# Linear attention with a gated FFN on one core: load gates read a ScalarE marker of each step instead of the newest FFN product

## The chip, the cores and the metric

The kernel runs on one core of a Trainium2 chip. The metric is the device time of one execution in microseconds: 285.78 us before the change (median of 3 runs, 285.7 to 285.8). A profiled execution, from whose trace all stretches below are read, spans 284.2 us between its first and its last instruction.

The core has five engines that run side by side, each through its own instructions in order: TensorE (PE in the profile; its weight loads are the row PEld), VectorE (DVE), ScalarE (ACT), GpSimd (POOL) and SyncE (SP). Transfers run on 16 DMA engines. An instruction that needs another engine's result waits for a semaphore, and all that stands behind it on its own engine waits too.

## The reference

```python
def phi(x, c, s):
    r = np.maximum(x, 0.0)
    return np.concatenate([r * c, r * s], axis=-1)
q_p = phi(q, cos_w, sin_w)
k_p = phi(k, cos_w, sin_w)
kv = np.einsum('bhsf,bhsd->bhfd', k_p, v)
z = np.sum(k_p, axis=2)
num = np.einsum('bhsf,bhfd->bhsd', q_p, kv)
den = np.einsum('bhsf,bhf->bhs', q_p, z)[..., None] + 1e-06
x = (num / den)            # to (B*S, H*D) = (4608, 512)
a = x @ w1
b = x @ w2
h = a * b @ w3
out = h @ w_out
```

q, k and v are 8 batches x 8 heads x 576 positions x 64. w1 and w2 are 512 x 1024, w3 is 1024 x 1024, w_out is 1024 x 512. All inputs and the output are float32.

## The kernel before

**Blocks and slots.** The FFN runs in nine blocks of 512 tokens (t=0 to 8), written by `ffn_groups` (line 426). A block of t=1 or more has 24 steps, called slots: 16 product slots (x times a piece of w1, `aT`, and x times the same piece of w2, `bT`, in turn, for eight pieces) and 8 output slots (four outputs of 128 tokens, two slots each). w3 times w_out is multiplied once, in t=0, as `w34b`, so an output is one product of `abT` with `w34b`. Slots 0 to 39 are t=0, and t begins at slot 16+24t: t=1 at 40, t=2 at 64, t=3 at 88, t=4 at 112, t=5 at 136, t=6 at 160, t=7 at 184, t=8 at 208.

In a product pair ScalarE copies the first product from PSUM to `asb` (line 470, one of three buffers) and VectorE multiplies it with the second into `abT` (line 475). There are four PSUM buffers `ffnps` for these. An output is copied by ScalarE (line 497) to `osb`, or, for the first ten pairs of outputs, to `kept`, which is stored much later.

**Attention between the slots.** At each slot the kernel calls what a hand-written plan has put there (`at`, `plan`, lines 522 to 543), and these instructions follow those of the slot on their engines. A batch of attention goes through: loads of k, v and q, each in two pieces (`load`, line 109: 64 partitions with 320 positions, then 64 with 256, converted to bf16); features of k and q on VectorE and ScalarE (lines 259 and 263); values copied by GpSimd (line 283); the product of keys and values (line 291) and its copy `kvs`; the transpose `qpT` of the query features by DMA (line 277, issued by SP); the numerator `pnum` on TensorE (line 349); its division (lines 359 to 361) into `xblk`; and the transpose of that into the block's input `xT` by DMA (line 383, SP). The plan gives slots for all of them: `kf` for key features, `vc` for values, `kv` for the key-value product, `qf` for query features, `nu` for numerators and the xT transpose behind each. A batch has five pieces of up to 128 positions, so five slots for each. For batches 4 to 7 all slots are given relative to a base: 101, 127, 153, 178. Batch b has 576 tokens and blocks have 512, so t=3 needs the first three pieces of batch 3, t=4 the first two of batch 4, t=5 the first two of batch 5, t=7 the first of batch 7.

**Loads and their gates.** All loads of k, v and q after the first batch, and the stores of `kept` and most of `osb`, are issued by GpSimd. Keys and values have one buffer, queries two. A load piece could be issued long before its slot, since GpSimd has little else to do. So each is put behind a gate (`behind`, line 525): GpSimd copies one column of a tile to `seen`, and can't do so before that tile is written. `plan_loads` (line 545) uses the newest `asb`, kept in `last_product` (lines 460 and 471); so do the ten late stores (lines 619 to 623). `plan_loads` is called ahead of `plan` for the same batch, so at a shared slot the load stands first.

Of the kernel before, what the change touches and what calls it, by code (L numbers as in the profile page):

```python
# [11 lines left out]
BF16 = mybir.dt.bfloat16  # L12
# [4 lines left out]
P = 128  # L17
# [3 lines left out]
ROWS = [128, 128, 128, 128, 64]  # L21
# [47 lines left out]
def kernel(  # L69
# [11 lines left out]
    nc = tc.nc  # L81
# [10 lines left out]
    sm = ctx.enter_context(tc.tile_pool(name="sm", bufs=3))  # L92
# [59 lines left out]
    zeros = const.tile([P, 512], BF16, name="zeros")  # L152
# [68 lines left out]
    def w34_mm(jp, part):  # L221
        if part == 0:
            w34_acc[jp] = ffn_tile()
        acc, w3T = w34_acc[jp], w3Ts[jp]
        for lc in range(4 * part, 4 * part + 4):
            nc.tensor.matmul(acc[:, :], lhsT=w3T[:, lc, :], rhs=woutb[:, lc, :],  # L226
                             start=(lc == 0), stop=(lc == 7))
        if part == 1:
            nc.scalar.copy(out=w34b[:, jp, :], in_=acc[:, :])


    def order_of(b):

        return [0, 1, 2, 3, 4] if b % 2 == 0 else [4, 0, 1, 2, 3]
# [5 lines left out]
    feat = {}  # L240
# [29 lines left out]
    def prep_k(b, c):  # L270
        features(b, feat_of(b)[0], raw[b, "k"], c)
# [149 lines left out]
    def ffn_tile():  # L421
        pool = ps_ffn[ffn_tiles[0] // 2 % 2]
        ffn_tiles[0] += 1
        return pool.tile([P, 512], FP32, name="ffnps")

    def ffn_groups(t):
        x = xT[t]
        abT = fsb.tile([P, 8, 512], BF16, name="abT", bufs=2)

        def products(out, w, jc, tok):  # L430
            for kc in range(4):
                nc.tensor.matmul(out, lhsT=w[:, kc, ts(jc, 128)], rhs=x[:, kc, tok],  # L432
                                 start=(kc == 0), stop=(kc == 3))

        def on_half(half):

            for pair in range(2):
                a, b = ffn_tile(), ffn_tile()
                if pair == 0 and t == 0:
                    for quarter in range(2):  # L440
                        for i in range(2):
                            for ps, w in ((a, w1b), (b, w2b)):
                                products(ps[:, ds(256 * i + 128 * quarter, 128)], w, i,
                                         ds(256 * half + 128 * quarter, 128))
                            if half == 0 and quarter == 0 and i == 0:
                                yield
                        if quarter == 0:
                            yield
                else:
                    for ps, w in ((a, w1b), (b, w2b)):  # L450
                        for i in range(2):
                            products(ps[:, ts(i, 256)], w, 2 * pair + i, ts(half, 256))
                        if w is w1b and (t == 1 or half == 0):
                            yield
                asb = fsb.tile([P, 512], BF16, name="asb")
                nc.scalar.copy(out=asb[:], in_=a[:, :])
                nc.vector.tensor_mul(out=abT[:, ts(pair, 2), ts(half, 256)],
                                     in0=asb[:].rearrange("p (i n) -> p i n", i=2),
                                     in1=b[:, :].rearrange("p (i n) -> p i n", i=2))
                last_product[:] = [asb]  # L460
                yield

        if t < 2:
            yield from on_half(0)
            yield from on_half(1)
        for jc in range(4 if t < 2 else 0, 8):
            aT = ffn_tile()
            products(aT[:, :], w1b, jc, slice(0, 512))
            asb = fsb.tile([P, 512], BF16, name="asb")
            nc.scalar.copy(out=asb[:], in_=aT[:, :])  # L470
            last_product[:] = [asb]
            yield
            bT = ffn_tile()
            products(bT[:, :], w2b, jc, slice(0, 512))
            nc.vector.tensor_mul(out=abT[:, jc, :], in0=asb[:], in1=bT[:, :])  # L475
            yield
        if t == 0:
            for jp in range(8):
                for part in range(2):
                    w34_mm(jp, part)  # L480
                    yield
            early.close()
            holds.append(ctx.enter_context(tc.tile_pool(name="hold", bufs=HELD,
                                                        reuse_waits="tile")))
        for ms in range(3 if t == NT - 1 else 4):
            ops = ffn_tile()
            for jc in range(8):
                nc.tensor.matmul(ops[:, :], lhsT=abT[:, jc, ts(ms, 128)], rhs=w34b[:, jc, :],  # L488
                                 start=(jc == 0), stop=(jc == 7))
                if jc == 3:  # L490
                    yield
            if ms % 2 == 0:
                if len(held) < HELD:
                    osb = holds[0].tile([P, 2, 512], FP32, name="kept")
                else:
                    osb = fsb.tile([P, 2, 512], FP32, name="osb", bufs=2)
            nc.scalar.copy(out=osb[:, ms % 2, :], in_=ops[:, :])  # L497
            if t == NT - 1:
                store(nc.sync, osb[:, ms % 2:ms % 2 + 1, :], 4 * t + ms, 1)
            elif ms % 2 == 1:  # L500
                if len(held) < HELD:
                    held.append((osb, 4 * t + ms - 1))
                else:
                    store(nc.gpsimd, osb[:, :, :], 4 * t + ms - 1, 2)
            yield
        if t == NT - 1:
            for half in range(2):
                cols = ts(half, 256)
                ops = ffn_tile()
                for jc in range(8):  # L510
                    nc.tensor.matmul(ops[:, 0:256], lhsT=abT[:, jc, ts(3, 128)],  # L511
                                     rhs=w34b[:, jc, cols], start=(jc == 0), stop=(jc == 7))
                nc.scalar.copy(out=osb[:, 1, cols], in_=ops[:, 0:256])  # L513
                store((nc.sync, nc.scalar), osb[:, 1:2, :], 4 * t + 3, 1, cols)
                yield
# [6 lines left out]
    def at(s, *calls):  # L522
        slots[s] += calls

    def behind(what):

        seen = sm.tile([P, 1], BF16, name="seen", bufs=1)
        nc.gpsimd.tensor_copy(out=seen[0:what.shape[0], :], in_=what)  # L528

    def feature_of(b, i, c):  # L530
        return feat[b][i][0:ROWS[c], c, 0, 0:1]

    def plan(b, kf, vc, kv, qf, nu, loads=None, xt=None):
        order = order_of(b)
        for i, c in enumerate(order):
            at(kf[i], lambda c=c: prep_k(b, c))
            at(qf[i], lambda c=c: prep_q(b, c))
            at(vc[i], lambda c=c: prep_v(b, c))
        for i, c in enumerate(order):
            at(kv[i], lambda c=c, i=i: kv_chunk(b, c, i))  # L540
        for i, c in enumerate(order):
            at(nu[i], lambda c=c: num(b, c))
            at(xt[i] if xt else nu[i], lambda c=c: x_tr(b, c))

    def plan_loads(b, when):

        for piece, s in zip([(n, half) for n in "kvq" for half in range(2)], when):
            def issue(piece=piece):
                behind(last_product[0][:, 0:1])
                load(b, *piece)  # L550
            at(s, issue)

    last_product = []

    for c in range(NCH):
        prep_k(0, c)
# [44 lines left out]
    for c, s in zip(order_of(1), (31, 32, 33)):  # L601
# [2 lines left out]
    plan(2, kf=(33, 35, 37, 39, 40), vc=(41, 42, 43, 44, 45), kv=(45, 46, 46, 47, 47),  # L604
         qf=(40, 41, 42, 43, 44), nu=(48, 50, 52, 54, 57))
    plan_loads(3, (51, 53, 55, 57, 59, 61))
    plan(3, kf=(58, 60, 62, 63, 65), vc=(62, 63, 64, 65, 66), kv=(72, 73, 73, 74, 74),
         qf=(67, 69, 71, 73, 75), nu=(75, 77, 79, 82, 85))

    bases = {4: 101, 5: 127, 6: 153, 7: 178}  # L610
    for b, base in bases.items():
        plan_loads(b, [base - 26 + s for s in (3, 5, 7, 9, 12, 14)])
        plan(b, kf=[base + s for s in (-16, -14, -12, -10, -9)],
             vc=[base + s for s in (-12, -11, -10, -9, -8)],
             kv=[base + s for s in (-3, -2, -2, -1, -1)],
             qf=[base + s for s in (-8, -6, -4, -2, 0)],
             nu=[base + s for s in (0, 2, 4, 7, 10)])

    for i in range(HELD):
        def put(i=i):  # L620
            behind(last_product[0][:, 0:1])
            store(nc.gpsimd, held[i][0][:, :, :], held[i][1], 2)
        at(166 + 4 * i, put)

    g = 0
    for t in range(NT):
        for _ in ffn_groups(t):
            for u in slots[g]:
                u()
            g += 1  # L630
# [31 lines left out]
```

## Time and profile before

| | |
|---|---|
| time | 285.78 us (285.7 to 285.8) |
| span of the profile | 284.2 us |
| TensorE busy | 253.0 us, 89% |
| VectorE, ScalarE, GpSimd busy | 137.9, 126.7, 91.9 us |
| mean granted TensorE clock | 0.952 |
| DMA | 41.01 MB, 144 GB/s |
| gate copies `seen<-asb` on GpSimd (line 528) | 46, 201 ns each |

Columns of a group or timeline line are engine, source line, operation, what is written and read, shapes and count; in brackets stands how long the engine was idle before it and what ended that. A wait line gives the waiting engine and line, what it waited for, then total us, times, and the longest. A chain line gives start, duration and what. The two digit rows of the page cut the span into 40 slices of 7.1 us, in tenths.

### The profile page before, as it was taken

The numbers are of one execution on the slowest core, as the hardware profiler recorded it, in microseconds if no ns is written. First come the engines' busy times: TensorE is split into PE (matmuls) and PEld (weight loads), VectorE is DVE, ScalarE is ACT, GpSimd is POOL, SyncE is SP. The second block draws the span as 40 slices with busy tenths as digits, with TensorE's granted clock in tenths as the row PEclk, the third lists the DMA queues.
The fourth block names the chain that finished last, engine by engine and source line by source line (L and its number), as shares of the span: only waits on it lengthen the run. The fifth ranks groups of instructions, "written<-read, shape, count | busy, mean of one in ns | idle before, by whom it ended". The sixth has DMA issues, their size and how long they took to land.

```text
span 284.2 us, 4962 instructions
## 1 busy us (share of the span) xinstructions
PE 253.0 (89%) x1867; PEld 133.3 (47%) x1867; DVE 137.9 (49%) x330; ACT 126.7 (45%) x218; POOL 91.9 (32%) x191
## 2 busy tenths in 40 slices
PE   8789999989999998999699949999868718999993
PEld 3577555649654543454245414454324303444442
DVE  6774736468772473465265614565524312521420
ACT  2774236758337624572456314663434301324331
POOL 8573403213064022504060302508246520454000
PEclk9999999999999999999989986999995966999999
DMA  8999999994699679978985994679998992767005
GB/s 192 187 194 205 206 208 144 196 123 74 132 147 169 77 124 166 137 137 119 149 96 97 144 124 59 82 148 162 167 196 211 174 248 74 164 155 237 0 17 131
DMA packets 83894, 41.01 MB, mean 144 GB/s; under 512 B 51488, under 2 KB 80416, under 8 KB 83872
## 3 DMA queue, kind: packets, MB, share of 16 engines
q0 software_dynamic: 35456, 27.20, 62.6%
q1 hardware_dynamic: 48256, 13.38, 31.6%
q8 instruction: 14, 0.23, 0.3%
q10 hardware_dynamic: 160, 0.13, 0.2%
q14 instruction: 8, 0.07, 0.1%
HBM read 38.80 MB, written 9.44 MB: 170 GB/s over the span
## 4 chain that ended last, share of the span: by engine, by line
PE 35%; DMA 19%; ACT 2%; issue 1%; DVE 1%; POOL 0%; ACTq 0%; SPq 0%; POOLq 0%
PE ffnps L432 26%; DMA xT<-xblk 9%; PE ffnps L488 6%; DMA qpT<-qp 4%; DMA qs<-in_q_dram 3%; DMA ks<-in_k_dram 3%; PE pnum L349 1%; PE pnum L291 1%; ACT asb L470 1%; ACT qp L263 0%; DVE kvs L297 0%; POOL out_dram L417 0%; ACT kvs L296 0%; PE ffnps L511 0%; ACT osb L513 0%
## 5 line engine op out<-in xcount | busy, mean ns | idle before, releaser
L432 PE MATMUL ffnps<-xT,w1b 128*128 128x512 bf16 (+2 forms) x336 | 78.6, 361 | 14.8 <-DMA xT<-xblk 12.9
L432 PE MATMUL ffnps<-xT,w2b 128*128 128x512 bf16 (+2 forms) x336 | 78.7, 361 | 4.6 <-DVE abT L475 4.6
L475 DVE TENSOR_TENSOR abT<-asb,ffnps 128x512 bf16<-128x512 bf16 x64 | 43.9, 685 | 65.1 <-PE ffnps L432 62.8
L488 PE MATMUL ffnps<-w34b,abT 128*128 128x512 bf16 x280 | 67.0, 384 | 0.0
L470 ACT CAST asb<-ffnps 128x512 bf16<-128x512 f32 x64 | 37.3, 583 | 65.8 <-PE ffnps L432 52.9
L432 PEld LDWEIGHTS <-w1b 128*128 128x128 bf16 x336 | 31.4, 100 | 45.3 <-DMA xT<-xblk 11.4
L432 PEld LDWEIGHTS <-w2b 128*128 128x128 bf16 x336 | 31.5, 100 | 34.7 <-issue 10.2
L528 POOL COPY seen<-asb 128x1 bf16<-128x1 bf16 x46 | 9.2, 201 | 96.4 <-ACT asb L470 96.4
L488 PEld LDWEIGHTS <-abT 128*128 128x128 bf16 x280 | 25.7, 99 | 26.6 <-issue 1.1
L263 ACT ACTIVATE qp<-qs,sinv 128x512 bf16<-128x512 bf16 (+2 forms) x40 | 28.0, 717 | 10.0 <-DMA qs<-in_q_dram 6.5
L361 DVE TENSOR_TENSOR xblk<-pnum,den 128x512 bf16<-128x512 f32 (+1 forms) x39 | 27.0, 691 | 1.4
L263 ACT ACTIVATE kp<-ks,sinv 128x512 bf16<-128x512 bf16 (+1 forms) x35 | 25.0, 722 | 3.7 <-DMA ks<-in_k_dram 3.7
L497 ACT COPY kept<-ffnps 128x512 f32<-128x512 f32 x20 | 11.7, 585 | 25.9 <-PE ffnps L488 25.9
L349 PEld LDWEIGHTS <-qpT 128*128 128x128 bf16 x320 | 15.2, 100 | 15.5 <-issue 5.1
L283 POOL COPY va<-vs 128x512 bf16<-128x512 bf16 (+1 forms) x30 | 17.6, 630 | 14.3 <-DMA vs<-in_v_dram 12.0
L349 PE MATMUL pnum<-kvs,qpT 128*128 128x65 bf16 x312 | 16.9, 196 | 3.8 <-DMA qpT<-qp 2.6
L497 ACT COPY osb<-ffnps 128x512 f32<-128x512 f32 x15 | 8.8, 585 | 24.6 <-PE ffnps L488 24.6
L259 DVE TENSOR_SCALAR qp<-qs,cosv 128x512 bf16<-128x512 bf16 (+1 forms) x40 | 14.3, 366 | 8.8 <-DMA qs<-in_q_dram 8.8
L359 DVE TENSOR_SCALAR den<-pnum 128x8 f32<-128x8 f32 (+1 forms) x39 | 6.4, 164 | 24.0 <-PE pnum L349 24.0
L259 DVE TENSOR_SCALAR kp<-ks,cosv 128x512 bf16<-128x512 bf16 (+1 forms) x35 | 15.8, 473 | 3.5 <-DMA ks<-in_k_dram 3.5
L417 POOL DMA_DIRECT2D out_dram<-osb x18 | 9.6, 536 | 20.3 <-ACT osb L497 19.2
L226 PE MATMUL ffnps<-woutb,w3T 128*128 128x512 bf16 x64 | 15.0, 379 | 0.0
(84 smaller groups left out, 196.1 us busy)
## 6 DMA issues: line engine op xcount, KB each, us to landing
out_dram<-kept POOLq DMA_DIRECT2D x10, 256.0 KB, 4.3
qs<-in_q_dram POOLq DMA_DIRECT2D x9, 256.0 KB, 7.8
ks<-in_k_dram POOLq DMA_DIRECT2D x7, 320.0 KB, 5.3
qs<-in_q_dram POOLq DMA_DIRECT2D x7, 320.0 KB, 9.0
vs<-in_v_dram POOLq DMA_DIRECT2D x7, 320.0 KB, 9.9
ks<-in_k_dram POOLq DMA_DIRECT2D x7, 256.0 KB, 6.0
vs<-in_v_dram POOLq DMA_DIRECT2D x7, 256.0 KB, 9.2
out_dram<-osb POOLq DMA_DIRECT2D x6, 256.0 KB, 4.3
```

What stands on the lines that cost most here:

```text
L226: nc.tensor.matmul(acc[:, :], lhsT=w3T[:, lc, :], rhs=woutb[:, lc, :], start=(lc == 0), stop=(lc == 7))
L259: nc.vector.tensor_scalar(out=dst[:R, c, :, 0:D], in0=src[:R, :, c, :], scalar1=0.0, scalar2=cosv[:R, at:at + 1], op0=ALU.max, op1=ALU.mult)
L263: nc.scalar.activation(out=dst[:R, c, 0:n, D:F], in_=src[:R, 0:n, c, :], func=ACTF.Relu, scale=sinv[:R, at:at + 1], bias=0.0)
L283: eng.tensor_copy(out=feat_of(b)[2][:R, c, :, 0:D], in_=raw[b, "v"][:R, :, c, :])
L349: nc.tensor.matmul(nt[:, h // 4, ds((h % 4) * 65, 65)], lhsT=qpT[:, h, ds(at, 128)], rhs=kvs[:, h, :], start=True, stop=True)
L361: nc.vector.tensor_tensor(out=xblk[rows], in0=n4[:, :, :, 0:D], in1=den[rows].unsqueeze(3).to_broadcast([R, 2, 4, D]), op=ALU.mult)
L417: on.dma_start(out=rows[:, :, cols], in_=osb[64 * i:64 * i + rows.shape[0], :, cols])
L432: nc.tensor.matmul(out, lhsT=w[:, kc, ts(jc, 128)], rhs=x[:, kc, tok], start=(kc == 0), stop=(kc == 3))
L470: nc.scalar.copy(out=asb[:], in_=aT[:, :])
L475: nc.vector.tensor_mul(out=abT[:, jc, :], in0=asb[:], in1=bT[:, :])
L488: nc.tensor.matmul(ops[:, :], lhsT=abT[:, jc, ts(ms, 128)], rhs=w34b[:, jc, :], start=(jc == 0), stop=(jc == 7))
L497: nc.scalar.copy(out=osb[:, ms % 2, :], in_=ops[:, :])
```

## The change

Each gate gets its own marker: ScalarE copies one element of a tile of zeros into `mark`, and GpSimd copies that. The marker depends on no data; it is ready when ScalarE, which works in order, has come to it, that is, after all that the slot and the slots before it gave ScalarE. The gate is thereby meant to follow the steps in every slot, and GpSimd no longer reads `asb`. The load pieces of batches 4 to 7 go one slot sooner, the first key features of batches 3 to 7 one slot later. `feature_of`, which nothing calls, and `last_product` go.

```diff
-                last_product[:] = [asb]
                 yield
...
             nc.scalar.copy(out=asb[:], in_=aT[:, :])
-            last_product[:] = [asb]
             yield
...
-    def behind(what):
-
+    def hold_back():
+
+        mark = sm.tile([P, 1], BF16, name="mark", bufs=8)
+        nc.scalar.copy(out=mark[0:1, :], in_=zeros[0:1, 0:1])
         seen = sm.tile([P, 1], BF16, name="seen", bufs=1)
-        nc.gpsimd.tensor_copy(out=seen[0:what.shape[0], :], in_=what)
+        nc.gpsimd.tensor_copy(out=seen[0:1, :], in_=mark[0:1, :])
...
             def issue(piece=piece):
-                behind(last_product[0][:, 0:1])
+                hold_back()
                 load(b, *piece)
...
-    plan(3, kf=(58, 60, 62, 63, 65), vc=(62, 63, 64, 65, 66), kv=(72, 73, 73, 74, 74),
+    plan(3, kf=(59, 60, 62, 63, 65), vc=(62, 63, 64, 65, 66), kv=(72, 73, 73, 74, 74),
          qf=(67, 69, 71, 73, 75), nu=(75, 77, 79, 82, 85))
...
-        plan_loads(b, [base - 26 + s for s in (3, 5, 7, 9, 12, 14)])
-        plan(b, kf=[base + s for s in (-16, -14, -12, -10, -9)],
+        plan_loads(b, [base - 26 + s for s in (2, 4, 6, 8, 11, 13)])
+        plan(b, kf=[base + s for s in (-15, -13, -11, -10, -9)],
...
         def put(i=i):
-            behind(last_product[0][:, 0:1])
+            hold_back()
             store(nc.gpsimd, held[i][0][:, :, :], held[i][1], 2)
```

More of the change, by code (lines that the diff above doesn't have):

```diff
@@ L523, in at @@
         slots[s] += calls
-    def behind(what):
+    def hold_back():
+        mark = sm.tile([P, 1], BF16, name="mark", bufs=8)
+        nc.scalar.copy(out=mark[0:1, :], in_=zeros[0:1, 0:1])
         seen = sm.tile([P, 1], BF16, name="seen", bufs=1)
-        nc.gpsimd.tensor_copy(out=seen[0:what.shape[0], :], in_=what)
-    def feature_of(b, i, c):
-        return feat[b][i][0:ROWS[c], c, 0, 0:1]
+        nc.gpsimd.tensor_copy(out=seen[0:1, :], in_=mark[0:1, :])
     def plan(b, kf, vc, kv, qf, nu, loads=None, xt=None):
@@ L548, in issue @@
             def issue(piece=piece):
-                behind(last_product[0][:, 0:1])
+                hold_back()
                 load(b, *piece)
             at(s, issue)
-    last_product = []
     for c in range(NCH):
```

## The prediction

> **What bounds the kernel now.** I read the page first: engine shares, slices, chain.
>
> ```profile
> span 284.2 us, 4962 instructions
> PE 253.0 (89%) x1867; PEld 133.3 (47%) x1867; DVE 137.9 (49%) x330; ACT 126.7 (45%) x218; POOL 91.9 (32%) x191
> ...
> PE   8789999989999998999699949999868718999993
> ...
> PEclk9999999999999999999989986999995966999999
> ...
> PE 35%; DMA 19%; ACT 2%; issue 1%; DVE 1%; POOL 0%; ACTq 0%; SPq 0%; POOLq 0%
> ```
>
> TensorE (PE) carries the kernel, and its holes lie late: slices 20, 24 and 29 to 33 (7.1 us each), with the granted clock down right after them. The chain names DMAs there. Next the waits of PE alone:
>
> ```profile
> PE ffnps L432 <- DMA xT<-xblk: 12.9, 3, 6.2
> PE ffnps L432 <- DVE abT L475: 4.6, 3, 3.5
> PE pnum L349 <- DMA qpT<-qp: 2.6, 1, 2.6
> PE ffnps L432 <- ACT kp L263: 1.3, 1, 1.3
> ```
>
> Three waits for the transposed attention output xT take 12.9 us. PE's timeline puts them at 137.2 to 139.9 (block t=4 begins, slot 112), 165.0 to 169.1 (t=5, slot 136) and 229.5 to 235.75 (t=7, slot 184); the 1.3 us is at 112.0 (t=3, slot 88). The chain of waits, cut to the first two, gives issue and landing:
>
> ```profile
> 130.99 8.76 DMA xT<-xblk
> 139.75 0.14 issue
> ...
> 159.21 9.15 DMA xT<-xblk
> 168.35 0.72 issue
> ```
>
> The least that an xT transpose takes to land, says the view of that tile, is 2.3 us. Why 8.8? GpSimd's (POOL's) timeline:
>
> ```profile
> 129.01 0.19 POOL L528 COPY seen<-asb 128x1 bf16<-128x1 bf16 x1 [9.72 <-ACT asb L470]
> 129.61 0.69 POOL L115 DMA_DIRECT2D ks<-in_k_dram  x1 [0.41 <-issue]
> 130.29 0.20 POOL L528 COPY seen<-asb 128x1 bf16<-128x1 bf16 x1
> 130.42 0.68 POOL L119 DMA_DIRECT2D ks<-in_k_dram  x1
> 131.09 0.20 POOL L528 COPY seen<-asb 128x1 bf16<-128x1 bf16 x1
> 131.21 0.68 POOL L115 DMA_DIRECT2D vs<-in_v_dram  x1
> 131.88 0.20 POOL L528 COPY seen<-asb 128x1 bf16<-128x1 bf16 x1
> 132.00 0.68 POOL L119 DMA_DIRECT2D vs<-in_v_dram  x1
> ```
>
> Four pieces, planned two slots apart, go out in 2.4 us. Only the first gate waited (9.72 us); the other three have no wait, for in the eight output slots of a block no new asb is made, and the newest is already there. A gate holds in the product slots and is open in the output slots, where the next block's xT leave. The same burst shows at 104.65 (five pieces) and 156.8 (three).
>
> **What the Trainium skill says.** "DMA: Bandwidth & Descriptors", Queues, rings and completion order: each DMA engine takes the queues in turn, a packet at a time, so loads and transposes share the engines. The trace agrees that they share, not that evenly: from 133 to 135 the load queue moved about 180 GB/s and the transposes nothing. Same page, Anatomy of one DMA: DMA engines don't wait on semaphores, waits happen on the issuing sequencer before dispatch; so the only brake on a burst is the gate in front of the issue. POOL's timeline shows just that. "TensorE: Matmul & The Clock Gate", Why this matters for your kernels: no idle gaps over about 3 us, or the clock halves. Here a gap of 2.67 us was followed by a clock of 0.67 (139.9 to 145.0), one of 1.29 us by none. "ScalarE: Activation LUTs", Rules for kernel authors, asks about 0.3 us per activation beside its elements; the trace has 0.203 us for one of 128x1 (line 169).
>
> **What the holes cost.** A product slot takes 0.863 us at full clock (starts 113.32, 114.18, 115.05). Past a hole I take start-to-start times over that. t=4: 2.67 idle, then four slots in 5.13 for 3.45: 1.68; sum 4.35. t=5: 4.07, then 6.63 for 3.70: 2.93; sum 7.0. t=3: 1.3. From 201 to 241 (t=6): idle 0.19+0.96 (key piece late), 3.48 (query piece late), 2.60 (qpT), 6.20 (xT), half clock 2.6+2.0; sum 18. All holes: 30.7 us, half clock included.
>
> **The change, part by part.**
> Marker: 46 ScalarE copies of one element. Nearest row 0.203 us; 46x0.203=9.3 us on ACT, busy 126.7 of 284. Behind each wait the next asb, hence the abT product and a PSUM buffer; PE runs some two slots (1.7 us) ahead of those, so 0.2 is hidden, save where ACT has just been held by a late piece. Bounds 0 and 9.3; I take 0.3. That POOL no longer reads asb frees ACT from waiting for POOL before it writes the third asb after (1.9 us in four waits, at most 0.6, none on PE's path): 0. POOL's copy stays, 0.2 us, beside PE's work.
>
> Gates: in an output slot the marker queues behind the last output copy on ACT, so it opens when that output is done. I read when the outputs end in PE's timeline and add 0.6 for the copy (0.585, line 497) and 0.5 for both markers with the time between (seen at 129.01, issue at 129.61). Issue and landing of single pieces are from the DMA view, asked in short stretches.
> Batch 5 (slots 103, 105, 107, 109 for 104, 106, 108, 110): the first gate opens on the block's last asb before and after, 129.6; then outputs 0, 1 and 2 end at 131.1, 133.1 and 135.1, so 132.2 for 130.4, 134.2 for 131.2, 136.2 for 132.0. The xT that t=4 needs is issued at 130.99 and PE gets to slot 112 at 137.2: 6.2 us of room. It will have one key piece ahead of it and one close behind, not four around it. Nearest rows: the xT of 104.07, with two pieces right behind, took 3.7 us; that of 77.57, with pieces 0.2 and 1.7 us behind, took 6.2. I take 5; t=4 wins its 4.35.
> Batch 6 (slots 129, 131, 133, 135): 160.0, 162.0, 164.0, 166.1 for 156.8, 157.6, 158.4, 172.2. Its xT leaves at 160.91, PE is there at 165.0: only 4.1 us of room, and it takes 3.7 to 6.2. Left over 0 to 2.1 idle; I take 1.5, and win 5.5.
> Batch 4: 102.5, 104.5, 107.3, 109.3, 111.0 (slots 77 to 86) for five in 104.65 to 108.5. The xT of 106.08 took 7.1; at 5.3 it is there before 112.0. Win 1.3.
> Batch 7 (in t=5's outputs and t=6): first key piece 191.6 for 193.7, as it no longer stands behind the store of outputs 0 and 1 in POOL's order; queries 199.8 and 201.7 for 203.5 and 205.8. But the DMA digits are 9 nearly throughout from 192 to 236, so what counts is the queue: the last query piece landed at 213.8 after 21 us without a gap, and the queue now starts 1 to 2 us sooner. The key wait (1.15) goes, the query wait grows into that room; net win 1 to 2.5, I take 1.5. The holes at 225.6 and 229.5, made by stores (a put at slot 178 now waits for an output, some 3 us later) and the same late queries, move along with it: 0.
>
> Key features one slot later, from slots base-16, -14, -12 to -15, -13, -11: the product of keys and values stands at base-3, eight slots off; 0. What the wait adds: POOL holds the later pieces, hence values and queries, in its order. The second value piece of batch 5 lands some 4 us later (about 141), needed by slot 115 at the earliest for a copy and 124 for PE: hidden. The query gates (slots 112 and 114) open on the same asb as before. Batch 4's first query piece goes out 3.5 us later and its second lands within 1.5 us of its feature, as it did (115.6 to 120.7): 0 to 3 over batches 4 to 6; I take 0.5.
>
> Sum: 1.3+4.35+5.5+1.5-0.3-0.5=11.85. 285.78-11.85=273.9.
>
> **Rivals.**
> Half: two queues share badly, and spaced pieces still push xT by 6 us; t=5 wins 2, t=4 2.7, t=3 1.3, t=6 1: 278.8. For it: the 6.2 at 77.57. Against: these lands come with 4 to 6 us of room.
> All: t=6 also opens, as the later put leaves room to the qpT of 216.9 (it took 11.3 us): 2.6 and half of xT and half clock there, some 7 more: 267. Against: the DMA queues were busy nearly all of 192 to 236, 44 us, where PE has work for 44-18=26.
> Nothing: DMA volume rules, each hole reappears as a wait for v or q: 285 to 286. Against: DMA digits have zeros in each of t=3 to t=5 (170 to 173 is empty).
> Slower: later queries, now behind spaced loads, stop ACT and DVE in batches 4, 5 and 6 as in 210.5 to 214, each 3.5 plus 1.7 at half clock: +15.6, while 12 are won: 289. For it: the features at slots 93 and 145 already wait 1 to 2 us for the last query piece (it landed at 120.7 and 183.2; the slots began at 117.6 and 180.0). Against: their gates open on the same asb, and less stands in the queue ahead.
>
> **How the numbers follow.** Forecast 0.56, half 0.18, all 0.10, nothing 0.06, slower 0.10. Likeliest time 273.9. The range goes down to all (267) and up past half, 282, which leaves out nothing and slower and a little else. Faster: 0.56+0.18+0.10 and half of nothing, 0.87; same 0.02; slower 0.11.
>
> **What would show it.** Right: POOL's copies of the mark each wait in the output slots, pieces some 2 us apart; xT in 3.7 to 6 us; no PE hole before t=4 and none over 2 us before t=5, clock full there; PE's wait for xT down from 12.9 to some 6 or 7, nearly all before t=7. Wrong: xT landing after 7 us though pieces are spaced; PE waiting on abT with ACT or DVE held by q in t=3 to t=5; ACT's own wait for marks; or a t=6 that loses its 18 us, which I don't expect.

## The result and the profile after

| | before | after |
|---|---|---|
| time, median of four executions | 285.74 us (282.42 to 285.80) | 274.81 us (272.61 to 279.45) |
| ratio of undisturbed runs | | 0.962, interval 0.952 to 0.972 |
| span of the profile | 284.2 us | 270.5 us |
| TensorE busy | 253.0 us | 244.5 us |
| ScalarE busy | 126.7 us | 130.4 us |

The kernel is 10.9 us faster by the medians; 11.85 were forecast. The profiled execution after is the fastest of its four (272.61 us) and the one before, at 286.33 us, is slower than its four, so the two traces lie 13.7 us apart, more than the medians. Executions of one kernel differ by some per cent here (the kernel before took 280 to 294 us over all chips used), which is why most verdicts below rest on the traces as well.

The page after. Rows as before: span, TensorE's slices, its granted clock, and the chain by engine.

```profile
span 270.5 us, 5000 instructions
...
PE   8789999999999999989999979995998619999993
...
PEclk9999999999999999999999999999899968999999
...
PE 64%; DMA 23%; ACT 4%; issue 4%; DVE 3%; POOL 1%; ACTq 0%; POOLq 0%
```

A slice is now 6.8 us. From slice 3 to slice 27 only slice 24 is below eight tenths (its hole of 1.4 us is read below), slice 28 has a new wait ahead of slot 160, and TensorE's share of the chain went from 35% to 64%. One deep hole is left, slices 32 and 33. TensorE's waits:

```profile
PE ffnps L432 <- DMA xT<-xblk: 11.0, 2, 8.2
...
PE ffnps L432 <- ACT asb L469: 1.5, 2, 1.1
PE ffnps L432 <- ACT mark L526: 1.4, 1, 1.4
...
PE pnum L349 <- DMA qpT<-qp: 0.6, 1, 0.6
```

The sum for xT hardly fell, 12.9 to 11.0, but it is made of other waits: 2.7 us ahead of slot 160 (new) and 8.25 us ahead of slot 184. The waits of 2.67 and 4.07 us ahead of slots 112 and 136 are gone or reduced to 1.4 us. That last one is booked on the marker; the xT of that block landed at 161.50 and the product started at 161.59, so it is a wait for xT too. GpSimd's timeline at the place shown before:

```profile
128.80 0.18 POOL L528 COPY seen<-mark 1x1 bf16<-1x1 bf16 x1 [9.19 <-ACT mark L526]
129.40 0.69 POOL L115 DMA_DIRECT2D ks<-in_k_dram  x1 [0.42 <-issue]
131.76 0.18 POOL L528 COPY seen<-mark 1x1 bf16<-1x1 bf16 x1 [1.68 <-ACT mark L526]
132.22 0.68 POOL L119 DMA_DIRECT2D ks<-in_k_dram  x1 [0.28 <-issue]
133.79 0.18 POOL L528 COPY seen<-mark 1x1 bf16<-1x1 bf16 x1 [0.90 <-ACT mark L526]
134.24 0.68 POOL L115 DMA_DIRECT2D vs<-in_v_dram  x1 [0.28 <-issue]
135.77 0.18 POOL L528 COPY seen<-mark 1x1 bf16<-1x1 bf16 x1 [0.85 <-ACT mark L526]
136.23 0.68 POOL L119 DMA_DIRECT2D vs<-in_v_dram  x1 [0.28 <-issue]
```

Each of these gates has a wait in brackets now, and the four pieces leave in 6.8 us instead of 2.4. Over the whole trace 39 of the 46 gates waited for ScalarE; before, 19 of 46 did. The xT issued at 130.69 landed after 5.7 us (before 8.8), and TensorE goes from the last numerator of t=3 into t=4 without a gap, 0.4 us after that landing:

```profile
136.50 0.42 PE L349 MATMUL pnum<-kvs,qpT 128*128 128x65 bf16 x8
136.76 1.02 PE L432 MATMUL ffnps<-xT,w1b 128*128 128x512 bf16 x3
```

Where the time went, from the starts of the blocks in the two traces:

| start of | before | after | ahead by |
|---|---|---|---|
| slot 88 (t=3) | 113.3 | 111.8 | 1.5 |
| slot 112 (t=4) | 139.9 | 136.8 | 3.1 |
| slot 136 (t=5) | 169.1 | 161.6 | 7.5 |
| slot 152 (outputs of t=5) | 187.0 | 177.0 | 10.0 |
| slot 160 (t=6) | 195.4 | 188.3 | 7.1 |
| slot 184 (t=7) | 235.8 | 222.3 | 13.4 |
| end | 284.2 | 270.5 | 13.7 |

### The profile page after: what moved, and what is told of

Its sections match the earlier page's. It is cut to its first block, busy times and chain, and to the rows that moved or that the text cites. A ratio compares the mean times of both kernels' runs of the same rounds, so it can differ in the third digit from the quotient of the medians.

```text
span 270.5 us, 5000 instructions
## 1 busy us (share of the span) xinstructions
PE 244.5 (90%) x1837; PEld 131.1 (48%) x1867; DVE 137.1 (51%) x330; ACT 130.4 (48%) x264; POOL 93.5 (35%) x191
## 4 chain that ended last, share of the span: by engine, by line
PE 64%; DMA 23%; ACT 4%; issue 4%; DVE 3%; POOL 1%; ACTq 0%; POOLq 0%
PE ffnps L432 34%; PE ffnps L486 18%; DMA w3b<-in_moe_w_dram 6%; DMA xT<-xblk 5%; DMA qs<-in_q_dram 5%; PE pnum L349 4%; PE ffnps L226 3%; DMA w2b<-in_moe_w_dram 3%; PE pnum L291 2%; DMA kf<-in_k_dram 2%; DMA qpT<-qp 2%; ACT kp L263 1%; ACT asb L469 1%; DVE kvs L297 1%; DVE xblk L361 1%
## 5 line engine op out<-in xcount | busy, mean ns | idle before, releaser
L432 PE MATMUL ffnps<-xT,w1b 128*128 128x512 bf16 (+2 forms) x324 | 75.6, 353 | 15.0 <-DMA xT<-xblk 11.0
L432 PE MATMUL ffnps<-xT,w2b 128*128 128x512 bf16 (+2 forms) x331 | 75.8, 353 | 0.2
L486 PE MATMUL ffnps<-w34b,abT 128*128 128x512 bf16 x270 | 64.8, 379 | 0.5
L528 POOL COPY seen<-mark 1x1 bf16<-1x1 bf16 x46 | 8.4, 182 | 106.6 <-ACT mark L526 106.6
L263 ACT ACTIVATE kp<-ks,sinv 128x512 bf16<-128x512 bf16 (+1 forms) x35 | 24.4, 718 | 0.1
L259 DVE TENSOR_SCALAR qp<-qs,cosv 128x512 bf16<-128x512 bf16 (+1 forms) x40 | 14.9, 381 | 6.3 <-DMA qs<-in_q_dram 6.1
L259 DVE TENSOR_SCALAR kp<-ks,cosv 128x512 bf16<-128x512 bf16 (+1 forms) x35 | 13.4, 405 | 1.4 <-DMA ks<-in_k_dram 1.3
L417 POOL DMA_DIRECT2D out_dram<-kept x24 | 12.7, 533 | 2.9 <-issue 2.9
```

Of the source, the lines that this page charges most:

```text
L259: nc.vector.tensor_scalar(out=dst[:R, c, :, 0:D], in0=src[:R, :, c, :], scalar1=0.0, scalar2=cosv[:R, at:at + 1], op0=ALU.max, op1=ALU.mult)
L263: nc.scalar.activation(out=dst[:R, c, 0:n, D:F], in_=src[:R, 0:n, c, :], func=ACTF.Relu, scale=sinv[:R, at:at + 1], bias=0.0)
L417: on.dma_start(out=rows[:, :, cols], in_=osb[64 * i:64 * i + rows.shape[0], :, cols])
```

## The experiments

The theory: loads were too close together in the output slots, because the gates were open there; closing them lets the transposes land in time. Rivals: the shifted slots do it; GpSimd's no longer reading `asb` does it; and for the large hole left in t=6, late queries against late stores. Each kernel ran six times, in five rounds beside the kernel before.

**Gates without the slots.** The changed kernel with three lines put back:

```diff
-    plan(3, kf=(59, 60, 62, 63, 65), ...
+    plan(3, kf=(58, 60, 62, 63, 65), ...
-        plan_loads(b, [base - 26 + s for s in (2, 4, 6, 8, 11, 13)])
-        plan(b, kf=[base + s for s in (-15, -13, -11, -10, -9)],
+        plan_loads(b, [base - 26 + s for s in (3, 5, 7, 9, 12, 14)])
+        plan(b, kf=[base + s for s in (-16, -14, -12, -10, -9)],
```

> The changed kernel with the old slots for loads and key features: the marker gates alone. Theory (closed gates in the output slots space the pieces): for batches 4 to 6 an old even slot and the new odd slot before it open on the same output copy, so nearly all of the gain stays, 275 to 278 us; PE's wait for xT at slot 112 is gone (0 to 1 us), at slot 136 at most 2 us. Batch 7's first key piece is behind the store again (before: 193.74), so the wait at slot 160 (2.7 us) goes and the query stall of t=6 (3.5 us) comes back. Rival (the shifted slots bring the gain): 284 to 286 us.

Measured 275.98 us (273.45 to 277.95), ratio to before 0.976, interval 0.966 to 0.985. Blocks t=3, t=4 and t=5 start at 111.7, 136.3 and 161.5 us, where the changed kernel has 111.8, 136.8 and 161.6. The gates alone bring the gain of these blocks, and a single wait for xT is left, the one ahead of slot 184:

```profile
PE ffnps L432 <- DMA xT<-xblk: 6.1, 1, 6.1
```

The slots show only for batch 7: the wait ahead of slot 160 is absent, a query stall stands in t=6 (3.57 us), and t=7 starts 2.4 us later than with the whole change.

**Slots without the gates.** The kernel before with the same three lines changed the other way.

> The kernel before with the new slots for loads and key features, gates on the newest asb as before. Theory: bursts stay in the output slots, and batch 6 now sends four pieces at once ahead of its xT instead of three: 284 to 288 us, PE's wait for xT 12 us or more, pieces 0.8 us apart. Rival (the slots bring the gain): 275 to 278 us.

Measured 285.57 us (284.01 to 287.98), no gain: the kernel before had a median of 285.3 in the same rounds, and the ratio is 1.016, interval 1.007 to 1.024. GpSimd at batch 6:

```profile
156.79 0.69 POOL L115 DMA_DIRECT2D ks<-in_k_dram  x1 [0.41 <-issue]
157.47 0.36 POOL L528 COPY seen<-asb 128x1 bf16<-128x1 bf16 x1
157.60 0.83 POOL L119 DMA_DIRECT2D ks<-in_k_dram  x1
158.27 0.35 POOL L528 COPY seen<-asb 128x1 bf16<-128x1 bf16 x1
158.39 0.84 POOL L115 DMA_DIRECT2D vs<-in_v_dram  x1
159.07 0.36 POOL L528 COPY seen<-asb 128x1 bf16<-128x1 bf16 x1
159.19 0.84 POOL L119 DMA_DIRECT2D vs<-in_v_dram  x1
```

Four pieces in 2.4 us, 0.8 apart, and TensorE then waits 5.13 us ahead of slot 136 instead of 4.07. Its waits:

```profile
PE ffnps L432 <- DMA xT<-xblk: 14.0, 4, 8.1
PE ffnps L432 <- issue: 5.1, 1, 5.1
```

The 5.1 us is the wait ahead of slot 136. It is booked on nothing, but the xT of that block landed at 170.04 and the product started at 170.13, so it comes on top of the 14.0. The slots by themselves bring no gain.

**A closed gate without a marker.** Slots as after, but the gate reads the newest copy that ScalarE made, be it of a product or of an output (the edit, cut to its main lines):

```diff
             nc.scalar.copy(out=asb[:], in_=aT[:, :])
+            last_product[:] = [asb[:, 0:1]]
...
             nc.scalar.copy(out=osb[:, ms % 2, :], in_=ops[:, :])
+            last_product[:] = [osb[:, ms % 2, 0:1]]
...
-                hold_back()
+                behind(last_product[0])
```

> No ScalarE marker: the gate reads one column of the newest product copy or output copy, at the new slots. Theory: what counts is that the gate closes in output slots, by whatever ScalarE result: within 1% of the changed kernel, 272 to 277 us, pieces 2 us apart. Rival (it matters that GpSimd no longer reads asb, so that ScalarE is not held): clearly slower than the changed kernel, 279 us or more.

Measured 273.5 us (272.54 to 274.19), ratio to before 0.970, interval 0.964 to 0.976. In its timeline the second to fourth gates of batch 5 wait for output copies:

```profile
131.65 0.19 POOL L529 CAST seen<-kept 128x1 bf16<-128x1 f32 x1 [1.68 <-ACT kept L497]
132.10 0.69 POOL L119 DMA_DIRECT2D ks<-in_k_dram  x1 [0.26 <-issue]
133.68 0.19 POOL L529 CAST seen<-kept 128x1 bf16<-128x1 f32 x1 [0.89 <-ACT kept L497]
134.13 0.69 POOL L115 DMA_DIRECT2D vs<-in_v_dram  x1 [0.26 <-issue]
```

Some 0.1 us ahead of the marker's times. So neither the marker as such nor GpSimd's reading of `asb` matters (it reads `asb` here): what counts is that the gate has something to wait for in an output slot.

**Four markers per gate.**

```diff
-        nc.scalar.copy(out=mark[0:1, :], in_=zeros[0:1, 0:1])
+        for _ in range(4):
+            nc.scalar.copy(out=mark[0:1, :], in_=zeros[0:1, 0:1])
```

> The changed kernel with four ScalarE markers per gate instead of one, so 138 more copies of 188 ns each (26 us on ScalarE). Theory (hidden behind PE, which runs ahead): 274 to 277 us, at most 2 us more than the changed kernel, as gates also open 0.4 us later. Rival (the marker is on the path to asb): every added copy counts, up to 300 us.

Measured 277.84 us (277.02 to 284.01): some 3 us above the changed kernel's 274.81 for 138 more copies, more than the 2 us allowed and far from 26. The cost isn't clean: VectorE's wait for queries rose to 16.6 us (6.1 after). Each gate opens later by three copies, so part of the 3 us may be later loads; no run tells the two apart. One marker per gate costs nothing that could be measured: see the pair with the late stores moved, below.

**The late stores moved.** The wait of 8.25 us ahead of slot 184 is the largest left. SyncE issued its xT at 214.18 and it took 8.1 us, with GpSimd's stores of `kept` and `osb` around it. A line of the chain of waits, then GpSimd's timeline:

```profile
214.18 8.11 DMA xT<-xblk
...
209.05 1.04 POOL L417 DMA_DIRECT2D out_dram<-kept  x2 [0.29 <-issue]
211.04 1.06 POOL L417 DMA_DIRECT2D out_dram<-osb  x2 [0.95 <-ACT osb L495]
212.94 0.18 POOL L528 COPY seen<-mark 1x1 bf16<-1x1 bf16 x1 [0.85 <-ACT mark L526]
213.41 2.09 POOL L417 DMA_DIRECT2D out_dram<-kept  x4 [0.29 <-issue]
```

The edit, to the changed kernel:

```diff
-        at(166 + 4 * i, put)
+        at(186 + 4 * i, put)
```

> The changed kernel with the ten late stores at slots 186 to 222 instead of 166 to 202. The wait of 8.25 us for xT ahead of slot 184 stands in a stretch where five of these stores (2.5 MB) share the DMA engines with the query and xT transposes. Theory (those stores hold the transposes up): the wait falls to 2 us or less and the half clock after it goes, 265 to 268 us. Rival (the late queries of batch 7 hold it up, as the prediction took stores and queries together): 271 to 274 us, a wait of 6 us or more stays.

Measured 265.16 us (264.55 to 267.01). The wait is gone; TensorE goes from the last output of t=6 into t=7 at once:

```profile
217.21 1.02 PE L486 MATMUL ffnps<-w34b,abT 128*128 128x512 bf16 x4
218.07 1.03 PE L432 MATMUL ffnps<-xT,w1b 128*128 128x512 bf16 x4
```

The same xT, issued at 214.57, took 3.2 us, as the view of transfers says:

```profile
xT<-xblk SPq DMA_TRANSPOSE x1, 3.2
```

The time alone doesn't prove it, for TensorE also came to slot 184 later than after the change: a query stall of 3.28 us, which the trace after doesn't have, stands in t=6 here. What speaks for the stores is the shorter landing, and that t=7 starts at 218.1 instead of 222.3 in spite of the stall. A cleaner pair follows with the queries, below.

The same edit on the kernel before:

> The kernel before with the ten late stores at slots 186 to 222: open gates in the output slots stay. If the last hole before slot 184 is the stores' alone, it goes here too: 276 to 279 us, with the waits ahead of slots 112 and 136 as they were (2.7 and 4 us). If late queries make it: 283 to 286 us.

Measured 274.39 us (271.34 to 275.91), better than expected: this one line, without the change, is worth as much as the change. Waits for xT ahead of slots 88, 112 and 136 are there as long as the gates are open (2.71, 1.86 and 4.03 us), and they are the only ones; the one ahead of slot 184 is gone:

```profile
PE ffnps L432 <- DMA xT<-xblk: 8.6, 3, 4.0
```

And on the kernel without a marker:

> Gates on the newest product or output copy, without a ScalarE marker, and the ten late stores at slots 186 to 222. Theory (both effects are separate): 263 to 267 us, as the markers' cost goes too (about 1 us).

Measured 265.12 us (263.74 to 266.49) beside 265.16 with markers, in the same rounds: the marker's price, which I had put at 1 us, is not seen in runs that spread over some 2.5 us. The holes of the two traces differ, though: without a marker a wait of 3.62 us ahead of slot 184 is left. Its xT left at 211.29, among six pieces of `osb` stores, and took 6.4 us. So moving the late stores shortens that hole, but doesn't close it in every kernel.

**Key features at their old slots.** The changed kernel with `kf` as before.

> The changed kernel with the key features at their old slots. Theory: eight slots of room to the key-value product, so no difference: 273 to 276 us. Rival (the later key features are needed since keys now land later): ScalarE and VectorE stand at the keys, PE waits on abT behind slots 137 and 163, 277 us or more.

Measured 275.72 us (273.89 to 278.59); the changed kernel has 274.81. No difference that these runs could tell, as expected, and no wait of TensorE for `abT` behind slots 137 and 163, which the rival asked for.

**Queries.** In the kernel with the late stores moved, TensorE's waits that are left lie behind queries or for xT. First, all pieces three slots sooner:

```diff
-        plan_loads(b, [base - 26 + s for s in (2, 4, 6, 8, 11, 13)])
+        plan_loads(b, [base - 26 + s for s in (-1, 1, 3, 5, 8, 10)])
```

> The changed kernel with the late stores at 186 to 222 and all load pieces of batches 4 to 7 three slots sooner still. What is left in the kernel with the late stores moved: waits behind the queries (0.96, 1.19 and 3.28 us, with half clock after the last) and for xT (1.15 and 2.43 us). Theory (a piece lands 5 to 7 us after its gate, the features come too early for it by 1 to 3 us): the waits for queries go, those for xT stay within 1 us: 259 to 263 us. Rival (earlier pieces meet the qpT and xT transposes instead): no gain or a loss, 265 to 270 us.

Measured 271.41 us (267.09 to 278.23), no gain over 265.16: the rival was right in kind. The profiled execution took 273.61 us, so its lengths are those of one of the longer runs. TensorE's query waits are gone, but the pieces now go out with the xT of the block boundary, which mostly take 6 to 8 us, and TensorE waits ahead of every block from t=3 to t=7 (1.73, 2.19, 3.26, 2.15, 2.23 us). Here sooner loads pay at the transposes for what they save at the features.

Second, the order of the pieces, keys, queries, values:

```diff
-    def plan_loads(b, when):
-
-        for piece, s in zip([(n, half) for n in "kvq" for half in range(2)], when):
+    def plan_loads(b, when, order="kvq"):
+
+        for piece, s in zip([(n, half) for n in order for half in range(2)], when):
...
-        plan_loads(b, [base - 26 + s for s in (2, 4, 6, 8, 11, 13)])
+        plan_loads(b, [base - 26 + s for s in (2, 4, 6, 8, 11, 13)], "kqv")
```

> The changed kernel with the late stores at 186 to 222 and the pieces of batches 4 to 7 in the order keys, queries, values. Theory (late queries hold ScalarE and VectorE, values have slack until the key-value product): the three waits behind queries go, 259 to 262 us. Rival (values then come too late for GpSimd's copies and the key-value product at base-3): TensorE waits there, 265 to 270 us.

Measured 260.24 us (259.16 to 263.85), ratio to the kernel before 0.916, interval 0.910 to 0.921: the best of all. TensorE is 94% busy and the clock full in every slice:

```profile
span 257.6 us, 4996 instructions
...
PE   8889999998999999999999998999699999999993
...
PEclk9999999999999999999999999999999999999999
```

The same order on the changed kernel, stores where they were:

> The changed kernel with the pieces of batches 4 to 7 in the order keys, queries, values; late stores as in the changed kernel. If the hole of 8.25 us ahead of slot 184 is the stores' alone, it stays at 6 us or more and only the waits behind queries go (1.13 and 0.41 us): 271 to 274 us. If late queries have a share in it, it shrinks to 4 us or less: 266 to 269 us.

Measured 273.07 us (270.93 to 274.21). TensorE is ahead of the changed kernel by 1.5 us at slot 136 and by 3.5 us at the first output of t=6, and then waits 12.29 us ahead of slot 184. From its chain of waits:

```profile
207.66 1.17 PE ffnps L486 x6
208.83 13.93 DMA xT<-xblk
222.76 0.05 issue
222.81 0.61 PE ffnps L432
```

The hole grew from 8.25 to 12.29 us and ends where it ended, at 222.8 for 222.3. With the stores moved and the same order of queries (the run before this one) t=7 starts at 211.2, with no wait: these two kernels differ by the late stores alone, and by 12.8 us in time. So the stores set the end of the hole; queries only set where it begins.

Last, batch 7 one slot later, against the 2.62 us left ahead of slot 160:

```diff
-        plan_loads(b, [base - 26 + s for s in (2, 4, 6, 8, 11, 13)], "kqv")
+        plan_loads(b, [base - 26 + s + (b == 7) for s in (2, 4, 6, 8, 11, 13)], "kqv")
```

> Late stores at 186 to 222, queries second, and the pieces of batch 7 one slot later, so that its first key piece stands behind the store of outputs 0 and 1 and not ahead of the xT of slot 153. Theory: the wait of 2.62 us for xT ahead of slot 160 goes, and no new one comes, since queries have room now: 256.5 to 259 us. Rival (the store ahead holds the later pieces, queries late again): 260 to 263 us.

Measured 261.39 us (258.89 to 263.21), no better than 260.24. That wait went, but two others came in t=6: 1.49 us behind `asb`, while ScalarE stood 2.35 us for the second key piece, and 2.14 us behind GpSimd's copies of values. The median lies in the rival's range, though the runs reach into both; of the rival's mechanism the trace has late pieces, but keys and values, not queries.

## Why the prediction was right, and where it was not

**Open gates in the output slots are the cause: shown.** The gates alone keep the gain of t=3 to t=5, the slots alone gain nothing, and a gate on the output copies does it without a marker. The mechanism needed nothing else.

**The steps for t=3 to t=5.** For t=3 1.3 us were forecast, 1.5 measured. For t=4, idle 2.67 and half clock 1.68: both gone, with xT landing in 5.7 us where 5 was taken; that left 0.4 us to spare. For t=5, 5.5 of 7.0 us were to be won, with 1.5 idle left over; 1.4 was left and the half clock went, so 5.6. The forecast times of the gates were within 0.5 us (132.2, 134.2 and 136.2 for batch 5, measured 132.22, 134.24 and 136.23).

**Queries a little too late.** I took 0.5 us over batches 4 to 6; the trace has holes of 1.13 us at 120.6 and 0.41 at 174.1. Batch 4's first query piece left at 111.28, as forecast, and landed after 7.7 us. So 1.54 us, inside the 0 to 3 given; the "slower" rival had hold of a real effect, at a tenth of its size.

**t=6, where the forecast was near for a wrong reason.** I forecast a net win of 1.5 us, with all holes moving along. By the table, 3.7 us were won from slot 152 to the end, out of larger parts of both signs. Gone: the waits at keys (1.15), the query stall (3.48) with its half clock (2.6), and 2.0 of the 2.6 us for qpT. New: 2.71 us for xT ahead of slot 160 and some 1.6 us at lower clock behind it (0.69 from 188.3 to 193.5). Grown: the xT wait ahead of slot 184, from 6.20 to 8.25. Two steps failed. The first is the key piece of batch 7: I had not looked at what it meets by leaving ahead of the store of outputs 0 and 1. The xT of slot 153, issued at 181.94, took 6.3 us (3.3 before), which is the new wait. My sign in the trace, a wait for xT of 6 or 7 us in sum, was wrong with it: it is 11.0.

The second is "the queue now starts 1 to 2 us sooner" and "the query wait grows into that room". The query pieces left at 194.19 and 196.14. TensorE was 10.0 us ahead at slot 152, so on the clock of the kernel before that is 204.2 and 206.1, and not the 199.8 and 201.7 of the forecast: no sooner than the 203.5 and 205.8 they had. They were in time because the first of them landed after 6.7 us (9.2 before) and TensorE itself had been held up at slot 160. That is not the change's merit. In the two traces with these load slots and half clock behind slot 160, this one and that with the old key slots, the first query piece took 6.7 and 5.3 us and TensorE has no query stall; in the four with full clock there (gates on outputs, four markers, late stores moved with and without a marker) it took 10.6 to 11.2 us and the stall is there, with 2.58, 3.65, 3.28 and 3.19 us. No run tests what ties the two together. So that the forecast for t=6 came within some 2 us is luck, and with it a part of the agreement of the whole sum. The traces lie 13.7 us apart and the medians 10.9, so the 11.85 is tested to some 2 us at best.

**Stores and queries in one.** I put the hole ahead of slot 184 on "stores and the same late queries", and "all" at 267 us on a later put at slot 178. That put did move, and the hole stayed. Moving all late stores out of t=6 took it away (265 us), in the kernel before as well (274 us), and earlier queries did not (273 us). With queries second, the late stores alone make the difference between a wait of 12.29 us and none. So the late stores set its end; what was left without a marker (3.62 us) stood among the stores of `osb`. My reason against "all", that the DMA queues were full for the whole stretch, was a fair reading; what it lacked is that five of the late stores need not be there.

**The marker.** 0.3 us taken, bounds 0 and 9.3. With and without it the medians are 265.16 and 265.12, with a spread of some 2.5 us each: the upper bound is excluded, 0.3 and 0 are not told apart. A marker took 0.188 us. The 0.3 us that the prediction quotes from "ScalarE: Activation LUTs" (Rules for kernel authors) is given there for an activation whose bias is read from a tile; the one at line 169, at 0.203 us, has a constant bias, so the two don't differ by what the prediction suggests.

**Key features.** Taken at 0, measured 0.9 us, with all runs inside the range of the changed kernel's: not told from 0.

What stays open: how much of the 3 us of four markers is ScalarE's time and how much the later gate; whether the pieces have to be spaced, or would do as well in one burst behind the xT, which no run tried; and why the kernel's executions spread over several per cent.

## What to carry to other kernels

A throttle that waits for a piece of data holds only where that data is being made: look in the timeline for gates without a wait in brackets, and give the gate something that every stage produces. When transfers share engines with a transfer that the critical path waits for, look for those that nobody waits for soon, here the late stores, and for the order among the others, here queries ahead of values; these two edits took the kernel from 274.8 to 260.2 us. A hole that ends at the same time however early the engine gets there belongs to what ends it.

## What the runs showed of the hardware

The prediction quotes from "TensorE: Matmul & The Clock Gate" (Why this matters for your kernels) that idle gaps over about 3 us halve the clock, and found 2.67 us enough. The runs show that the length of a gap doesn't decide. In the kernel with gates on outputs and late stores moved, gaps of 3.19 and 3.62 us were followed by full clock; with all pieces sooner, one of 2.16 us was followed by half clock.

What decides is how the gap falls. In each of the 14 traces the granted clock changes only at points of a grid of 3.413 us, whose first point lies 3.8 to 6.7 us after the start of the span, differently in each trace. TensorE's idle time, counted in each stretch of that grid:

| kernel | gap | idle in the stretches it fell in | clock in the stretch behind each |
|---|---|---|---|
| before | 137.22 to 139.89, 2.67 us | 0.33, 2.34 | 1.00, 0.50 |
| slots alone | 112.89 to 116.17, 3.29 us | 1.85, 1.44 | 1.00, 1.00 |
| gates on outputs, late stores moved | 200.74 to 203.93, 3.19 us | 1.55, 1.69 | 1.00, 1.00 |
| the same | 214.14 to 217.76, 3.62 us | 1.81, 1.81 | 1.00, 1.00 |
| late stores moved | 186.00 to 188.43, 2.43 us | 1.12, 1.32 | 1.00, 1.00 |
| late stores moved, pieces sooner | 193.63 to 195.79, 2.16 us | 0.15, 2.05 | 1.00, 0.50 |

Of 986 stretches at full clock (without the last 10 us of each trace) 25 had 2.03 us of idle time or more, and the next one ran at half clock each time. The other 961 had 1.85 us at most, and the next one ran at full clock each time. So in these traces a gap that is split between two stretches can cost nothing beyond itself, and a shorter one almost wholly inside one stretch is followed by 3.4 us at half clock. The prediction priced the half clock as a fixed part of each hole; it depends on where the grid lies.
